# ScalarE's share and order of work in the first row of an attention and mixer kernel, and a float64 conversion by absolute value, limit, shift and sign

## The chip, the cores and the metric

One core of a Trainium2 chip. The metric is the device time of one execution in microseconds (us). The kernel before took 1377.46 us (median of three runs, 1377.15 to 1379.82). "PE" in a profile is TensorE, "PEld" its weight loads, "DVE" VectorE, "ACT" ScalarE, "POOL" GpSimd, "SP" SyncE, which only issues transfers here ("SPq").

## The reference, cut to what matters

```python
# q, k, v: (8, 8, 576, 64) float32; tau = 0.02
scores = np.matmul(q, k.transpose(0, 1, 3, 2)) / 8.0
thresh = np.max(scores, axis=-1, keepdims=True) - tau
scores = np.where(scores >= thresh, scores, -1e9)
attn = softmax(scores)                       # along the last axis
x = (attn @ v) -> (B=8, S=576, H*D=512)      # heads side by side
# mixer; its weights are float64
u = x + (relu(x^T @ w_tok1) @ w_tok2)^T      # 576 -> 256 -> 576
out = u + relu(u @ w_ch1) @ w_ch2            # 512 -> 1536 -> 512
```

The reference's weights are float64, the kernel works in float32. So the kernel also converts each weight itself, from the two 32-bit words of a float64.

## The kernel before

The kernel goes over the attention in iterations `u`, nine to a pair of head pairs, 18 to a batch row. The first row (u = 0 to 17) has nothing else for TensorE to do; later rows fill TensorE's gaps with the mixer of the row before. In iteration `u` it computes scores of `u`, normalizes `u-1` and turns (transposes) unit `u-2`. The first row's turns are made by TensorE, nine blocks of 128x128 in three thirds, into PSUM tiles that share two banks:

```python
def turn(u, third):
    ...
    ps = ps_tr.tile(...)                       # two banks, three thirds
    for c in range(3):
        nc.tensor.transpose(out=ps[:, c, :], in_=e[:, k0 : k0 + P], identity=ident)
    on = nc.scalar.copy if third == 1 and u % 2 else nc.vector.tensor_copy
    on(out=eTs[key][:, 3 * third : 3 * third + 3, ...], in_=ps)
```

Every third iteration of the first row (u = 5, 8, 11, 14, 17) also multiplies three turned units with the values ("iterations with values"; the others I call plain). One iteration in the order of the program, cut:

```python
scores(u)                        # TensorE; then VectorE's maxima, GpSimd's bias
...
    last = values_due(u)         # TensorE, in iterations with values
norm(u - 1)                      # VectorE's reciprocal, GpSimd's scaling
weight_to(2.25 * (u - 1.5))      # conversion steps (first row)
while copies: copies.popleft()() # VectorE copies the values' result to xT
for i in range(3): turn(w, i)    # w = u - 2
...
weigh(u)                         # ScalarE: Prelu with the threshold, Exp
weight_to(2.25 * (u - 1))        # conversion steps
if t in when: load_qk(...)       # issue loads of q and k for later heads
if t == 2: prep(n + 1)           # VectorE transposes q and k (also at t == 7)
```

The conversion is cut into 31 pieces of three steps. A step has work for ScalarE (two steps), VectorE (three), GpSimd (an addition of the two words), and it issues the load of a later piece:

```python
def on_scalar(i, part):   # lo, hi: the two words of each float64
    part 0: lo = int(lo * 2^-29)                  # lower word, rounded
    part 1: h2 = Square(hi as float32)
def on_vector(i, part):
    part 0: bits = (hi << 3) & 0x3FFFFFFF         # tensor_scalar
    part 1: bits = (hi & 0xC0000000) | bits       # two tensors
    part 2: dst  = (h2 >= 2^-30) * dst            # two tensors
def weight(n):            # for each of the next n steps
    if part == 0: on_gpsimd(i - 1); load_piece(i - 1 + NRAW)
    else:         on_scalar(i + 1, part - 1)
    on_vector(i, part)
```

## Time and profile before

| what | before |
|---|---|
| time | 1377.46 us |
| TensorE busy after 200 us | 974 of 980 us |
| TensorE busy in the first 200 us | 157 of 200 us |
| second row starts (scores of u = 18) | 104.20 us |

The slices, the table by stretch and the timelines that the argument starts from are shown in the prediction. The conversion's VectorE work on full pieces (columns: line, engine, operation, tiles, forms, count | busy us, mean ns | idle just before, and what ended most of it):

```profile
L205 DVE SCALAR_TENSOR_TENSOR wc<-scratch,wc 128x512 uint32<-128x512 uint32 x24 | 24.2, 1009 | 0.6
L209 DVE SCALAR_TENSOR_TENSOR wc<-h,wc 128x512 f32<-128x512 f32 x24 | 20.0, 832 | 1.1
L201 DVE TENSOR_SCALAR wc<-scratch 128x512 uint32<-128x512 uint32 x24 | 14.2, 590 | 1.8 <-DMA scratch<-in_moe_w_ch_dram 1.8
```

The means lie far above the medians that the prediction quotes (702, 692 and 412 ns for all 26 full pieces): the same step takes up to 1.7 us when GpSimd works at the same time. Three waits between 14 and 200 us (columns: who, for whom: us in total, times, longest):

```profile
ACT eT L355 <- PE tr L353: 23.2, 7, 6.1
PE tr L353 <- DVE eT L355: 17.7, 8, 3.6
DVE mx L307 <- PE sc L302: 10.5, 10, 2.2
```

The second is TensorE's transposes that wait until VectorE has copied a turn's third out of the bank they need. The first is ScalarE idle before its copies, the third VectorE idle before its maxima.

### The profile page before, as it was taken

What the parts mean: (1) busy time and instruction counts of PE and PEld (TensorE: products, weight loads), DVE (VectorE), ACT (ScalarE), POOL (GpSimd) and SP (SyncE); (2) the same over time, 40 slices, a digit from 0 to 9 for tenths busy, and PEclk for the clock granted to TensorE, in tenths of its full rate; (3) what the DMA queues carried; (4) which work ended last, traced back from release to release, by engine and by line L of the source; (5) the groups of instructions that cost most, each with busy time, mean ns of one, the idle gap of its engine ahead of it and who ended that gap; (6) DMA issues with size and microseconds to landing.
All of it is one profiled execution on the core that took longest, in us unless ns stands there. A gap on an engine that the chain in (4) does not pass through costs nothing.

```text
span 1375.1 us, 17691 instructions
## 1 busy us (share of the span) xinstructions
PE 1322.7 (96%) x6226; PEld 817.9 (59%) x6226; DVE 588.2 (43%) x1017; ACT 581.8 (42%) x1288; POOL 356.0 (26%) x683
## 2 busy tenths in 40 slices
PE   6877799999999999999999999999999999999998
PEld 3444465646565666565665567565656576575675
DVE  6788875445444443434244444434333453201000
ACT  5666654454445444443434444353333444120110
POOL 4555653222222222222122222222121222100000
PEclk9988999999999999999999999999999999999999
DMA  5434655454544354433344435434433442400000
GB/s 121 98 96 125 183 142 124 100 123 98 122 109 114 82 121 94 113 88 95 77 100 94 113 77 123 106 83 98 103 87 75 107 103 63 115 1 16 8 11 21
DMA packets 278871, 128.20 MB, mean 93 GB/s; under 512 B 200896, under 2 KB 271552, under 8 KB 278784
## 3 DMA queue, kind: packets, MB, share of 16 engines
q1 hardware_dynamic: 150176, 111.06, 32.0%
q10 hardware_dynamic: 128608, 16.01, 7.3%
q8 instruction: 50, 0.82, 0.3%
q14 instruction: 37, 0.30, 0.1%
HBM read 43.25 MB, written 9.44 MB: 38 GB/s over the span
## 4 chain that ended last, share of the span: by engine, by line
PE 85%; DVE 7%; DMA 2%; SPq 2%; ACT 1%; issue 1%; POOL 1%; ACTq 0%; DVEq 0%; POOLq 0%
PE c L486 26%; PE c L470 26%; PE sc L302 11%; PE pv L413 9%; PE t L441 5%; PE t L448 3%; PE pv L408 3%; DVE mx L307 2%; SPq L374 2%; PE tx L432 1%; PE c L482 1%; DMA eT<-T 1%; PE tr L353 1%; DVE wc L205 1%; ACT e L317 1%
## 5 line engine op out<-in xcount | busy, mean ns | idle before, releaser
L307 DVE TENSOR_REDUCE mx<-sc 128x1 f32<-128x576 f32 x288 | 204.5, 751 | 487.9 <-PE sc L302 487.5
L470 PE MATMUL c<-xT,wc 128*128 128x256 f32 (+1 forms) x1920 | 399.4, 362 | 2.1 <-DVE xT L452 1.2
L486 PE MATMUL c<-wc,g 128*128 128x512 f32 x864 | 390.5, 597 | 0.0
L470 PEld LDWEIGHTS c<-xT,wc 128*128 128x128 f32 x1920 | 334.5, 191 | 71.5 <-issue 27.6
L308 POOL TENSOR_SCALAR bias<-mx,toff 128x1 f32<-128x1 f32 x288 | 82.8, 288 | 799.3 <-DVE mx L307 742.3
L317 ACT ACTIVATE e<-sc,bias 128x576 f32<-128x576 f32 x288 | 199.6, 739 | 162.0 <-POOL bias L308 161.4
L486 PEld LDWEIGHTS c<-wc,g 128*128 128x128 f32 x864 | 157.8, 190 | 175.7 <-issue 174.0
L471 ACT ACTIVATE g<-c 128x256 f32<-128x256 f32 (+1 forms) x240 | 86.7, 362 | 334.1 <-PE c L470 317.9
L324 ACT ACTIVATE e<-e,ntau 128x576 f32<-128x576 f32 x288 | 220.7, 771 | 0.0
L335 POOL TENSOR_SCALAR e<-e,rr 128x576 f32<-128x576 f32 x288 | 215.6, 761 | 15.8 <-DVE rr L332 4.3
L302 PE MATMUL sc<-kT,qT 64*128 64x288 f32 (+1 forms) x1280 | 196.6, 447 | 11.1 <-DVE kT L284 7.1
L365 DVE STREAM_TRANSPOSE T<-e 128x1152 f32<-128x1152 f32 x126 | 172.1, 1366 | 6.3 <-DMA eT<-T 2.6
L302 PEld LDWEIGHTS sc<-kT,qT 64*128 64x128 f32 (+1 forms) x1280 | 107.4, 184 | 98.3 <-issue 59.1
L413 PE MATMUL pv<-eT,lv 128*64 128x384 f32 (+1 forms) x1024 | 136.8, 409 | 0.0
L413 PEld LDWEIGHTS pv<-eT,lv 128*64 128x64 f32 x1024 | 76.1, 138 | 51.0 <-issue 43.6
L491 DVE COPY o<-c 128x512 f32<-128x512 f32 x36 | 24.9, 692 | 177.5 <-PE c L486 177.5
L418 ACT COPY xT<-pv 128x384 f32<-128x384 f32 (+1 forms) x56 | 21.0, 401 | 157.5 <-PE pv L413 157.5
L448 PE MATMUL t<-w,a 128*128 128x288 f32 x256 | 75.2, 421 | 7.2 <-DVE xT L452 5.3
L441 PE MATMUL t<-x_sb,w 128*128 128x512 f32 x160 | 72.1, 598 | 0.0
L448 PEld LDWEIGHTS t<-w,a 128*128 128x128 f32 x256 | 45.6, 191 | 32.2 <-issue 11.4
L452 DVE TENSOR_TENSOR xT<-xT,t 128x288 f32<-128x288 f32 x64 | 28.2, 446 | 80.5 <-PE t L448 80.0
L324 ACT ACTIVATION_READ_ACCUMULATOR e<-e,ntau 128x1 f32 x288 | 56.5, 196 | 0.0
(44 smaller groups left out, 554.7 us busy)
## 6 DMA issues: line engine op xcount, KB each, us to landing
eT<-T SPq DMA_DIRECT2D x672, 108.0 KB, 2.2
scratch<-in_moe_w_ch_dram SPq DMA_DIRECT2D x24, 512.0 KB, 3.7
lv<-in_v_dram SPq DMA_DIRECT2D x32, 288.0 KB, 3.3
out_dram<-o SPq DMA_DIRECT2D x36, 256.0 KB, 2.2
lk<-in_k_dram ACTq DMA_DIRECT2D x111, 72.0 KB, 2.6
lq<-in_q_dram ACTq DMA_DIRECT2D x106, 72.0 KB, 2.3
lq<-in_q_dram SPq DMA_DIRECT2D x22, 72.0 KB, 3.2
lk<-in_k_dram SPq DMA_DIRECT2D x17, 72.0 KB, 3.3
```

The lines of the kernel that those rows point to most:

```text
L302: nc.tensor.matmul(sc[h][rows, f, 0:HS], lhsT=qT[r, cols], rhs=kT[r, HS * f : HS * f + HS], start=True, stop=True)
L307: nc.vector.tensor_reduce(out=mx[:, c], in_=sc[h][:, :, 0:HS], axis=AX.XY, op=ALU.max)
L317: nc.scalar.activation(out=eh, in_=sc[h][:, :, 0:HS], func=AF.Prelu, bias=bias[:, h : h + 1], scale=SCALE, alpha=STEEP)
L324: nc.scalar.activation(out=eh, in_=eh, func=AF.Exp, bias=ntau, accum_out=rs[:, h : h + 1])
L335: nc.gpsimd.tensor_scalar(out=eh, in0=eh, scalar1=rr[:, h : h + 1], scalar2=1.0, op0=ALU.mult, op1=ALU.mult)
L365: nc.vector.transpose(out=T[:, :, place, :].rearrange("p a (c x) -> p c a x", c=NK), in_=e.rearrange("p (c a x) -> p c a x", c=NK, a=4))
L413: nc.tensor.matmul(to[r], lhsT=lv[:, j, :], rhs=e[j], start=False, stop=(c == NI - 1), skip_group_check=True)
L441: nc.tensor.matmul(ps, lhsT=w1[:, t, P * m : P * m + P], rhs=x_sb[:, t, :], start=(t == 0), stop=(t == NT - 1))
L448: nc.tensor.matmul(ps, lhsT=s["a"][:, m, P * c : P * c + P], rhs=w2[:, m, HS * f : HS * f + HS], start=(m == 0), stop=(m == NTK - 1))
L470: nc.tensor.matmul(ps, lhsT=wc1[:, j, c, :], rhs=uT[:, c, GR * i : GR * i + n], start=(c == 0), stop=(c == NCC - 1))
L471: nc.scalar.activation(out=s["g"][:, j, 0:n], in_=ps, func=AF.Relu)
L486: nc.tensor.matmul(flat, lhsT=s["g"][:, j, P * t : P * t + P], rhs=wc2[:, j, :], start=False, stop=(j == NJ - 1), skip_group_check=True)
```

## The change

Three parts. (a) ScalarE copies the middle third of every turn, not only of odd units. (b) In the first row's iterations with values, more conversion steps and ScalarE's Prelu and Exp stand ahead of the turns in the program, so that these engines work while TensorE multiplies the values. (c) The conversion is done another way: absolute value of the upper word (ScalarE), limit from below and multiply by 2^16, shift by 3, then put the sign in. It has one two-tensor step where it had two. The prediction's (d) is a consequence of (c): VectorE's first step of a piece now needs ScalarE's result.

```diff
@@ on_scalar
-                nc.scalar.activation(out=h2, in_=hi.bitcast(F32), func=AF.Square)
+                nc.scalar.activation(out=h2, in_=hi.bitcast(F32), func=AF.Abs)
@@ on_vector
             if part == 0:
+                nc.vector.tensor_scalar(out=h2, in0=h2, scalar1=2.0**-15, scalar2=2.0**16, op0=ALU.max, op1=ALU.mult)
+            elif part == 1:
                 nc.vector.tensor_scalar(
-                    out=bits, in0=hi, scalar1=3, scalar2=0x3FFFFFFF, op0=ALU.logical_shift_left, op1=ALU.bitwise_and
+                    out=bits, in0=h2.bitcast(U32), scalar1=3, scalar2=0, op0=ALU.logical_shift_left, op1=ALU.bitwise_or
                 )
-            elif part == 1:
-                nc.vector.scalar_tensor_tensor(
-                    out=bits, in0=hi, scalar=0xC0000000, in1=bits, op0=ALU.bitwise_and, op1=ALU.bitwise_or
-                )
             else:
-                nc.vector.scalar_tensor_tensor(out=dst, in0=h2, scalar=2.0**-30, in1=dst, op0=ALU.is_ge, op1=ALU.mult)
+                nc.vector.scalar_tensor_tensor(
+                    out=bits, in0=hi, scalar=0x80000000, in1=bits, op0=ALU.bitwise_and, op1=ALU.bitwise_or
+                )
@@ turn
-        on = nc.scalar.copy if third == 1 and u % 2 else nc.vector.tensor_copy
+        on = nc.scalar.copy if third == 1 else nc.vector.tensor_copy
@@ main loop
+        visit = False
         if due and not in_blocks(due[0][1]):
+            visit = due[0][0] <= u
             last = values_due(u)
...
-            weight_to(2.25 * (u - 1.5))
+            weight_to(2.25 * (u - (1 if visit else 1.5)))
+            if visit and on:
+                weigh(u)
...
-        if on:
+        if on and (b_now or not visit):
             weigh(u)
```

## The prediction

> **What bounds the kernel now.** I read the page's slices first, to see where TensorE is not full; then a table by stretch; then TensorE's timeline and waits inside the stretch that is not full; then VectorE's and ScalarE's timelines of single iterations.
>
> ```profile
> PE   6877799999999999999999999999999999999998
> DVE  6788875445444443434244444434333453201000
> PEclk9988999999999999999999999999999999999999
> ```
>
> Each digit is a slice of 34.4 us. TensorE is at 9 from the sixth slice on, and VectorE is high only before that. The same by stretch (columns: window, then busy us of PE, PEld, DVE, ACT, POOL, then PE clock, DMA share, GB/s):
>
> ```profile
> 0.00:104.00 104.00, 78.73 (x444) 47.77 (x444) 77.20 (x165) 64.75 (x135) 55.00 (x101) 0.92 0.46 104
> 104.00:125.00 21.00, 14.95 (x65) 8.32 (x63) 18.62 (x33) 15.46 (x31) 11.82 (x15) 0.67 0.58 147
> 125.00:200.00 75.00, 63.39 (x310) 40.82 (x307) 65.45 (x97) 46.82 (x97) 45.92 (x52) 0.98 0.58 154
> 200.00:1180.00 980.00, 974.35 (x4662) 597.23 (x4661) 416.05 (x708) 432.54 (x969) 243.26 (x518) 1.00 0.44 100
> ```
>
> After 200 us TensorE is busy 974 of 980 us: VectorE or ScalarE time saved there is worth nothing. All the change can win lies in the first 200 us, where TensorE idles 43 us (25.3 + 6.1 + 11.6) and runs below full clock. That caps the gain: 2% of 1377.5 is 27.5 us, nearly two thirds of all that idle time. The first row (18 iterations, turned on TensorE) ends at about 120 us; the weights' conversion ends at 200.
>
> What TensorE waits for in the first row (start, length, engine, what, idle before and what ended it), here seven last transposes of a turn:
>
> ```profile
> 29.60 0.55 PE L353 MATMUL tr<-ident,e 128*128 128x128 f32 x3 [2.31 <-DVE eT L355]
> 42.12 0.55 PE L353 MATMUL tr<-ident,e 128*128 128x128 f32 x3 [1.32 <-DVE eT L355]
> ...
> 55.13 0.55 PE L353 MATMUL tr<-ident,e 128*128 128x128 f32 x3 [0.57 <-ACT eT L355]
> 60.87 0.55 PE L353 MATMUL tr<-ident,e 128*128 128x128 f32 x3 [3.03 <-DVE eT L355]
> 74.25 0.55 PE L353 MATMUL tr<-ident,e 128*128 128x128 f32 x3 [2.18 <-DVE eT L355]
> ...
> 90.45 0.55 PE L353 MATMUL tr<-ident,e 128*128 128x128 f32 x3 [0.57 <-ACT eT L355]
> 95.96 0.90 PE L353 MATMUL tr<-ident,e 128*128 128x128 f32 x3 [2.53 <-DVE eT L355]
> ```
>
> The turns' PSUM has two banks and a turn has three thirds, so the last third waits for an earlier copy. Where ScalarE copies the middle third (odd units), the wait is 0.57 us and it is ScalarE's copy that ends it: the last third takes the middle one's bank. Where VectorE makes all three (even units), the wait is 1.3 to 3.0 us, because VectorE gets to its first copy only after two maxima, the sum's reciprocal and a conversion step. Seven plain even iterations wait 0.44 + 2.31 + 1.32 + 3.03 + 2.18 + 2.53 + 2.33 = 14.1 us.
>
> The iterations with values are different: there VectorE and ScalarE wait for TensorE, and do what could have been done meanwhile afterwards. The end of the last one:
>
> ```profile
> 103.90 0.48 ACT L355 COPY eT<-tr 128x384 f32<-128x384 f32 x1 [5.83 <-PE tr L353]
> 104.28 1.38 ACT L317 ACTIVATE e<-sc,bias 128x576 f32<-128x576 f32 x2
> 104.78 0.68 DVE L205 SCALAR_TENSOR_TENSOR wc<-scratch,wc 128x512 uint32<-128x512 uint32 x1
> 105.57 0.69 DVE L209 SCALAR_TENSOR_TENSOR wc<-h,wc 128x512 f32<-128x512 f32 x1
> 106.18 1.42 DVE L307 TENSOR_REDUCE mx<-sc 128x1 f32<-128x576 f32 x2
> ```
>
> ScalarE idles 5.8 us before its copy with its two Prelu behind it, though their bias was ready; VectorE puts two steps between its last copy and the next maxima, which are on the loop.
>
> **What the Trainium skill says.** "VectorE: DVE Perf Modes", section "The perf-mode tier table": fp32 `tensor_scalar` from SBUF to SBUF reaches two results a cycle, two-tensor work one. The trace agrees, on bit operations too: a 128x512 TENSOR_SCALAR has a median of 412 ns, SCALAR_TENSOR_TENSOR 702 and 692.
>
> "SBUF — State Buffer", section "Who interferes with whom": VectorE and GpSimd share a port pair, held for a whole instruction, wanted by two-input operations and by the two-port mode. The trace fits: the same three steps take up to 1516, 1676 and 1600 ns beside GpSimd's work. So the cheaper step does not escape the lock.
>
> "ScalarE: Activation LUTs", section "Table sets": abs is filler in every set, so no table load. Square takes 661 ns (median); the page has one rate for all functions, so I expect the same for the absolute value.
>
> "TensorE: Matmul & The Clock Gate", section "What's actually happening": idling lowers the clock, activity releases it. The trace shows 0.67 to 0.92 where TensorE idles and 1.00 after. Less idling may thus also shorten the matmuls; I count little for it, since when it switches cannot be read from here.
>
> **The change part by part.**
>
> (a) ScalarE copies the middle third in every turn: nine copies of 0.55 us leave VectorE (nominally 5 us), nine of 0.48 us go to ScalarE. The larger effect is the bank: the last third then follows ScalarE's early copy as in odd units. The seven waits would shrink to 0.57 each: 14.1 - 4.0 = 10.1 us of TensorE idle removed. But the loop then runs at VectorE's pace. Per even iteration VectorE loses the middle copy (about 0.5) and the gap before the last copy (0.17 to 0.53), plus what it waits for scores that now come earlier (0 to 0.6): about 1.0 us each, 7 us in all. I take 7, not 10.
>
> (b) Work ahead of the turns, in five iterations with values. In the one shown the next maxima can start when their first scores are there, about 105.3 instead of 106.18: 0.9. After the first one I read 0.8 in the same way; the one at 61 has one step of 0.42 less: 0.4; the one at 79 has a step of 0.68 behind a middle copy of 0.5, but the scores come at 88.5 against maxima at 89.17: 0.65; the one at 46 about 0.5. Sum 3.3. ScalarE's earlier Prelu frees the score banks sooner; the scores right after odd such iterations take 2.05 to 2.11 us, where others at full clock take 1.25. This overlaps with the same loop, so it adds perhaps 0.3: 3.6.
>
> (c) Conversion: Square becomes Abs (no cost), a bit TENSOR_SCALAR becomes one with max and multiply (0.41 for 0.41), one SCALAR_TENSOR_TENSOR of 0.69 becomes a TENSOR_SCALAR of 0.41, the other stays. So 0.28 us for each of 26 full pieces and about 0.15 for the five small ones: 8 us of VectorE time. In the first row the shortened step is on the loop in about five plain iterations: 5 x 0.28 = 1.4, of which I keep 1. In the second row (18 pieces, 5 us) half falls into the lock behind GpSimd's addition: 1.
>
> (d) What it adds: VectorE's first step now needs ScalarE's Abs, where it needed only the load. In the first row Abs mostly comes a call earlier: no wait that I can find. From the second row on Abs and the first step are in the same call, and ScalarE then often stands behind a Relu that waits for TensorE. At 148.70 the step would wait for an Abs that ends at about 149.1, and an addition that TensorE waits 2.19 us for stands behind it: 0.3 to 0.4 lost. Two or three of these: -1.
>
> Sum: 7 + 3.6 + 1 + 1 - 1 = 11.6 us. 1377.5 - 11.6 = 1366, -0.8%.
>
> **The rivals.**
>
> R1, VectorE's throughput takes the place of the wait. It is already busy 77 of the first 104 us and 84 of the next 96. If the even iterations merely trade the wait at the last third for a wait at the next scores or maxima, (a) is worth its nine copies at most where VectorE has no slack, some 3 us, and the whole about 6: 1371. For it: VectorE often runs without a gap from the last copy to the next maxima. Against it: the removed copy and the removed gap both lie in that very run.
>
> R2, the new dependency costs more than it gives: VectorE is in order, so a late Abs also delays maxima, copies and the additions that TensorE waits for. With 1 us lost in each of the nine second-row iterations that convert, the gain falls to about 4: 1373. For it: ScalarE waits 13.6 us there for weight loads, and VectorE did not wait for most of those. Against: the delayed step often would have stood in the lock anyway (the one after it takes 1.66 us where GpSimd's addition runs), so a delay there is partly free.
>
> R3, the clock joins in: with shorter gaps the first row stays at full clock. An iteration with values that ran at 0.78 took 7.9 us, the one at 1.00 took 6.6, with much the same work. Four of them a us faster, plus (a) at its full 10: 1358.
>
> R4, nothing: gains end in the wait for weight loads before 200 us, as these are issued behind VectorE's transposes' 16 DMAs on one queue. Against it: those loads move forward with the steps that issue them. 1376.
>
> **Range and chances.** R1 and R2 pull to 1371-1373, R3 to 1358. I take 1366, with 1358 to 1374 for eight in ten. Faster by over 2% would need 1350 or less, so two thirds of the idle time in 200 us: 0.03. Slower by over 2% would need 27 us of new waits in a stretch where each is bounded by a few: 0.005. The rest, 0.965, is within 2%.
>
> **What would show it.** (a) is right if no last third of a plain even turn waits over 1 us for VectorE's copy, and the wait of transposes for VectorE's copies (17.7 us on TensorE) falls below 8. (b) is right if ScalarE's 23.2 us of waiting before its copies goes to where its Prelu are already done, and the maxima follow the last copy with no step between them. (c) is right if the two TENSOR_SCALAR have a median near 0.41 us and the full conversion's VectorE time falls by about 8 us. (d) is right if VectorE waits for Abs under 4 us in all. After 200 us (less the gain) nothing may differ. The prediction is wrong if the first iteration of the second row starts less than 6 or more than 15 us earlier than before (104.2 us), or if what is won there is lost again before TensorE is full.

## The result, and the profile after

The changed kernel takes 1372.28 us (median of six runs, 1370.45 to 1375.01); the kernel before took 1379.57 in the same rounds (six runs, 1377.15 to 1383.88). The ratio is 0.9946, 95% interval 0.9924 to 0.9967: within 2%. The ratios here are worked out from the runs of the same rounds. They are not quite the ratios of the medians or of the plain means (for no_a below, the plain means give 0.9969). At -0.54% the gain is 7.4 us of the 11.6 predicted. The time lies inside the range, 6 us above its middle.

The trace taken with that result is of the slowest of its six runs, and in it the first scores start at 8.88 us against 7.06 before, because a first load landed late. A second set of runs (whole_again, below) gave a trace that starts at 7.06 us like the one of before. I use that second trace: span 1366.8 us against 1375.1. It is of the fastest of its six runs (1368.63 us), and the trace of before is of a run (1376.94 us) as fast as that kernel's fastest, so both show a somewhat better case than the medians do. Its slices of 34.2 us:

```profile
PE   6877899999999999999999999999999999999998
DVE  5878764445453543434334354434333443201000
PEclk9999999999999999999999999999999999999999
```

TensorE's fifth slice is at 8 where it was at 7, and the clock no longer falls to 8. By stretch, in the prediction's windows and columns:

```profile
0.00:104.00 104.00, 76.99 (x463) 48.44 (x463) 78.28 (x169) 75.19 (x157) 58.78 (x105) 0.98 0.48 111
104.00:125.00 21.00, 15.36 (x72) 8.69 (x72) 17.86 (x29) 13.37 (x27) 13.00 (x15) 0.84 0.56 158
125.00:200.00 75.00, 63.82 (x303) 40.11 (x302) 56.92 (x96) 45.87 (x97) 40.29 (x53) 1.00 0.59 155
200.00:1180.00 980.00, 974.22 (x4688) 597.31 (x4687) 413.26 (x700) 429.00 (x963) 240.40 (x512) 1.00 0.43 99
```

After 200 us nothing differs: TensorE is busy 974.22 us where it was 974.35. In the first 104 us TensorE does more work (463 instructions in the trace where there were 444) in less busy time, because its clock is 0.98 where it was 0.92, and ScalarE is busy 75.2 us where it was 64.8. The second row starts 6.07 us earlier (in the first trace, of the slowest run, at 103.68 us and so only 0.52 us earlier):

```profile
98.13 2.07 PE L303 MATMUL sc<-kT,qT 64*128 64x288 f32 x8
```

The last thirds of the plain even turns, which waited 0.4 to 3.0 us for VectorE, now wait for ScalarE's copy: 0.57 us in four of the seven, 0.82 to 1.37 us in three, 5.8 us in all for 14.1 before (shown are iterations 4, 6, 10, 12 and 16; line numbers are one higher than before):

```profile
27.86 0.55 PE L354 MATMUL tr<-ident,e 128*128 128x128 f32 x3 [0.82 <-ACT eT L356]
38.62 0.55 PE L354 MATMUL tr<-ident,e 128*128 128x128 f32 x3 [0.57 <-ACT eT L356]
...
56.94 0.55 PE L354 MATMUL tr<-ident,e 128*128 128x128 f32 x3 [1.37 <-ACT eT L356]
66.81 0.55 PE L354 MATMUL tr<-ident,e 128*128 128x128 f32 x3 [0.57 <-ACT eT L356]
...
87.80 0.55 PE L354 MATMUL tr<-ident,e 128*128 128x128 f32 x3 [1.33 <-ACT eT L356]
```

The waits between 14 and 200 us, those that answer to the three of before and the new one for the absolute value:

```profile
DVE mx L308 <- PE sc L303: 16.5, 10, 4.4
...
ACT eT L356 <- PE tr L354: 13.0, 10, 2.8
...
PE tr L354 <- ACT eT L356: 10.2, 12, 1.4
...
DVE h L202 <- ACT h L194: 8.6, 4, 4.0
...
PE tr L354 <- DVE eT L356: 5.0, 1, 5.0
```

TensorE's wait for VectorE's copies fell from 17.7 us to 5.0 (and that one is in the second row), while its wait for ScalarE's copies grew from 3.1 to 10.2. VectorE's wait for scores grew from 10.5 us to 16.5, but most of that in the second row: up to 125 us it grew from 5.5 to 7.4. And the conversion's VectorE work:

```profile
L208 DVE SCALAR_TENSOR_TENSOR wc<-scratch,wc 128x512 uint32<-128x512 uint32 x24 | 19.8, 824 | 0.4
L204 DVE TENSOR_SCALAR wc<-h 128x512 uint32<-128x512 uint32 x24 | 17.1, 713 | 0.7
L202 DVE TENSOR_SCALAR h<-h 128x512 f32<-128x512 f32 x26 | 15.8, 609 | 8.6 <-ACT h L194 8.6
```

All the conversion's steps together took VectorE 70.7 us between 14 and 200 us before, and 63.2 now. ScalarE's step costs the same (median 671 ns for Abs, 662 for Square), and both traces have one table load, as the prediction expected.

The length of iterations, from one scores' start to the next (iteration 2 from the second half of its scores), summed by kind:

| iterations | before | after | |
|---|---|---|---|
| plain, even (2, 4, 6, 10, 12, 16) and 18 | 37.80 us | 28.48 us | -9.3 |
| plain, odd (3, 7, 9, 13, 15) and 19 | 27.53 us | 27.79 us | +0.3 |
| with values (5, 8, 11, 14, 17) | 38.23 us | 40.38 us | +2.2 |

So the even iterations gave more than the 7 us I had put on part (a), and the iterations with values, on which part (b) works, became longer; iteration 17 alone, with 2.5 us, makes more than all of that. But single traces of this kernel differ by some 3 us in this stretch (first loads land between 7.06 and 8.9 us, clocks differ), so which part does what has to come from times.

### The profile page after: what moved, and what is told of

Same layout as the page of the kernel before. It is cut to its first block, busy times and chain, and to the rows that moved or that the text cites. A ratio compares the mean times of both kernels' runs of the same rounds, so it can differ in the third digit from the quotient of the medians. Undisturbed runs are those within 1.5% of the kernel's fastest.

```text
span 1373.2 us, 17692 instructions
## 1 busy us (share of the span) xinstructions
PE 1320.2 (96%) x6226; PEld 817.9 (60%) x6226; DVE 575.9 (42%) x1008; ACT 586.0 (43%) x1297; POOL 354.6 (26%) x683
## 4 chain that ended last, share of the span: by engine, by line
PE 86%; DVE 5%; DMA 3%; SPq 2%; ACT 1%; issue 1%; POOL 1%; ACTq 0%; DVEq 0%; POOLq 0%
PE c L471 26%; PE c L487 26%; PE sc L303 11%; PE pv L414 9%; PE t L442 5%; PE t L449 3%; PE pv L409 3%; DVE mx L308 2%; SPq L375 2%; PE tx L433 1%; PE c L483 1%; DMA eT<-T 1%; PE tr L354 1%; DMA lk<-in_k_dram 1%; DVE wc L208 1%
## 5 line engine op out<-in xcount | busy, mean ns | idle before, releaser
L303 PE MATMUL sc<-kT,qT 64*128 64x288 f32 (+1 forms) x1280 | 193.2, 441 | 12.5 <-DVE kT L285 8.9
```

The source lines that it names most:

```text
L303: nc.tensor.matmul(sc[h][rows, f, 0:HS], lhsT=qT[r, cols], rhs=kT[r, HS * f : HS * f + HS], start=True, stop=True)
```

## The experiments

Twelve kernels ran, each in six runs (a_last_third in five), in three sets of rounds, each set on one chip. All gave correct results.

| kernel | parts | median us | before, same rounds | ratio | 95% interval |
|---|---|---|---|---|---|
| whole_again | a b c | 1371.64 | 1379.44 | 0.9937 | 0.9914 to 0.9960 |
| a_only | a | 1374.64 | 1379.44 | 0.9960 | 0.9936 to 0.9984 |
| b_only | b | 1382.52 | 1379.44 | 1.0010 | 0.9984 to 1.0036 |
| c_only | c | 1377.06 | 1379.44 | 0.9978 | 0.9956 to 1.0001 |
| no_a | b c | 1374.35 | 1378.76 | 0.9976 | 0.9958 to 0.9993 |
| no_b | a c | 1371.03 | 1378.76 | 0.9942 | 0.9930 to 0.9954 |
| no_c | a b | 1375.05 | 1378.76 | 0.9974 | 0.9959 to 0.9988 |
| abs_early | a b c, ScalarE's steps earlier | 1374.63 | 1378.76 | 0.9969 | 0.9956 to 0.9981 |
| a_last_third | a on another third | 1394.34 | 1381.68 | 1.0098 | 1.0080 to 1.0115 |
| load_first | a b c, one load earlier | 1370.76 | 1381.68 | 0.9920 | 0.9898 to 0.9941 |
| both_early | a b c, load and copies earlier | 1370.48 | 1381.68 | 0.9918 | 0.9902 to 0.9934 |
| ac_both_early | a c, load and copies earlier | 1370.87 | 1381.68 | 0.9925 | 0.9908 to 0.9942 |

### Each part alone

The theory was my own sum (a 7, b 3.6, c and d 1 together); the rivals were that VectorE's pace takes (a) away, that (b) does nothing, and that the new dependency costs more. The whole, unchanged:

> The change once more, to have it in the same rounds as its parts, and a second trace, as the first one was taken of the slowest of its runs (its first scores came 1.8 us late, on a load). Expected: -7 us against the kernel before (ratio 0.995). If the trace starts as early as that of before, the first scores of the second row should come 3 to 6 us earlier than 104.2.

Measured: 0.9937, beside 0.9946 in the first rounds; so the whole gains 0.54 to 0.63%, 7.4 to 8.7 us.

Part (a) alone is the kernel before with one line changed:

```diff
-        on = nc.scalar.copy if third == 1 and u % 2 else nc.vector.tensor_copy
+        on = nc.scalar.copy if third == 1 else nc.vector.tensor_copy
```

> Only ScalarE's copy of the middle third in every turn. Theory BANK (a as predicted): the seven last thirds of even plain turns stop waiting for VectorE; -4 to -7 us. Rival PACE (VectorE's rate takes the wait's place): -1 to -3 us. A cost of its own: in iterations with values ScalarE's Prelu now stands behind the copy in all five, not in three, so the gain may be lower than with the reordering.

Measured: 0.9960, so -0.40%, 5.5 us. Less than 7 and more than the 3 of the rival. In its trace the even iterations take 33.0 us for 37.8 before, and the odd ones 22.4 for 19.0 (3, 7, 9, 13 and 15). So part of what the removed waits gave came back, but not as the rival had it: 3.2 of these 3.4 us are in iterations 9 and 15, which follow the two even iterations with values (8 and 14). It is the cost that was expected besides: ScalarE now waits there for the middle third, and its Prelu stand behind that copy. Iteration 8 in a_only:

```profile
52.74 0.48 ACT L355 COPY eT<-tr 128x384 f32<-128x384 f32 x1 [3.55 <-PE tr L353]
53.03 2.11 PE L302 MATMUL sc<-kT,qT 64*128 64x288 f32 x8
53.11 1.38 ACT L317 ACTIVATE e<-sc,bias 128x576 f32<-128x576 f32 x2
```

Before, the Prelu of iteration 8 started at 50.09 us, ahead of the turn, and the next scores took 1.25 us for these 2.11. In the changed kernel, where (b) puts the Prelu ahead of the turns, both iterations are back at 3.1 us (4.2 and 5.2 in a_only).

Part (b) alone is the kernel before with the four edits of the main loop in the diff above (`visit`, `weight_to`, and `weigh(u)` twice):

> Only the reordering in the five iterations with values. As predicted: -3.6 us. If the middle copy on ScalarE is what makes it pay, or if the steps moved ahead fall into GpSimd's lock before the copies, it is 0 to -2.

Measured: 1.0010, with 1.000 well inside its interval. The 3.6 us of the prediction (0.9974) lie outside it. How this came is read below.

Part (c) alone is the kernel before with the edits of `on_scalar` and `on_vector`:

> Only the conversion by absolute value. As predicted (c and d): -1 us. If the wait for Abs costs more (8.8 us of VectorE's time in the changed kernel's trace after 104 us), +1 to +3 us; if that wait only stands in the place of others, -2 to -3.

Measured: 0.9978, so -0.22%, 3 us, with 1.000 just inside its interval.

### All parts but one

To see whether parts overlap or help each other, the change with one part undone. The diffs are those above, backwards.

> The change without ScalarE's copy in even turns. If the parts simply add up (alone they gave -0.4%, +0.1% and -0.2%), this gives -0.1%, -1.5 us. If a is needed for b to pay (even turns then hold VectorE's loop), no less; if b is worth something only beside a, about -3 us would speak for it being c alone.

> The change without the reordering. Adding up: -0.6% (-8.5 us), as much as the whole or a little more; then b was worth nothing at all. If b serves a (as ScalarE's copy now stands before Prelu in every iteration with values), less: -5 us.

> The change with the old conversion. Adding up: -0.3% (-4 us). If c is needed, as three steps in one call take 0.28 us less each in iterations with values, -3; if b pays beside a, -6.

Measured: 0.9976, 0.9942 and 0.9974. With these, each part has four pairs of kernels that differ in it alone (for the whole I take the mean of its two measurements, 0.99415; some pairs compare ratios from different sets of rounds, and so from different chips):

| part | on nothing | on one other | on one other | on both others | mean |
|---|---|---|---|---|---|
| a | -0.40 | -0.36 (on b) | -0.36 (on c) | -0.35 | -0.37% |
| b | +0.10 | +0.14 (on a) | -0.02 (on c) | -0.01 | +0.05% |
| c | -0.22 | -0.18 (on a) | -0.34 (on b) | -0.33 | -0.27% |

In us of 1379.6: (a) -5.1, (b) +0.7, (c) with its dependency (d) -3.7; the sum is -8.1, and the whole measured -7.4 to -8.7. Each mean is good to about 0.15% or 2 us (an estimate: the intervals' half widths are 0.12 to 0.26%, and a mean is made of eight such ratios). So, as far as these intervals tell, the parts add up, each is worth the same whatever stands beside it, and (b) is worth nothing: the change without (b) is as fast as the whole. That the times add up does not mean that the traces do; see the end of the next section.

### Why part (b) gives nothing

Two things are in the trace of b_only. First, what the shorter path from the last copy to the next maxima is worth. In the iteration after the first one with values the kernel before has (scores, and VectorE's maxima of them, after two conversion steps):

```profile
37.96 2.05 PE L302 MATMUL sc<-kT,qT 64*128 64x288 f32 x8
...
39.70 1.42 DVE L307 TENSOR_REDUCE mx<-sc 128x1 f32<-128x576 f32 x2 [0.22 <-issue]
```

and with (b), where the two steps are done earlier:

```profile
37.98 1.25 PE L302 MATMUL sc<-kT,qT 64*128 64x288 f32 x8
38.08 0.56 DVE L355 COPY eT<-tr 128x384 f32<-128x384 f32 x1 [0.64 <-PE tr L353]
39.73 1.42 DVE L307 TENSOR_REDUCE mx<-sc 128x1 f32<-128x576 f32 x2 [1.08 <-PE tr L353]
```

The maxima start at 39.73 us, after a wait of 1.08 us, where they started at 39.70 without it. The steps stood in time that VectorE had to wait anyway. (The profile puts this wait down to a transpose behind the scores; why the maxima do not start at 39.3 is not clear.) From the scores' start to the maxima's the five iterations that follow one with values took 1.74, 1.34, 2.26, 1.34 and 1.98 us before, and 1.75, 1.34, 1.93, 1.34 and 1.34 with (b). At full clock 1.34 us is what eight score matmuls take before the maxima can start, and two iterations were already there. What is won is 0.33 + 0.64 = 1.0 us, where the prediction had 3.3.

Second, what it costs. A step moved ahead of the turns also stands ahead of VectorE's copy of the values' result, which TensorE waits for. Iteration 8 before:

```profile
50.90 0.61 DVE L420 COPY xT<-pv 128x192 f32<-128x192 f32 x2
...
51.66 0.92 PE L353 MATMUL tr<-ident,e 128*128 128x128 f32 x6 [0.47 <-DVE xT L420]
```

and in b_only:

```profile
51.05 0.47 DVE L209 SCALAR_TENSOR_TENSOR w<-h,w 128x288 f32<-128x288 f32 x1
51.44 0.61 DVE L420 COPY xT<-pv 128x192 f32<-128x192 f32 x2
...
52.20 0.92 PE L353 MATMUL tr<-ident,e 128*128 128x128 f32 x6 [1.10 <-DVE xT L420]
```

The copy starts 0.54 us later (0.72 counted from the iteration's start) and TensorE waits 1.10 us where it waited 0.47. In that trace the five iterations with values take 40.2 us for 38.2 before, but 1.4 of these 2.0 us are in iteration 17, where TensorE waits 0.34 us for the copy as before and one group of its matmuls takes 2.59 us for 1.47 at a lower clock (0.50 and 0.66 where it was 0.85 and 1.00). So alone (b) wins about 1 us behind these iterations, and what it surely loses in them is less than 1.

Beside (a), and so in the changed kernel, both sides are larger. Iterations 6, 9, 12 and 15, which follow one with values, take 17.9 us in no_b and 12.4 in whole_again; the five with values take 36.1 and 40.4. With the two mends described further below it is the same (17.9 and 12.4, 33.2 and 38.3 us in ac_both_early and both_early). From the scores' start to the maxima's hardly anything changes there: 6.29 and 5.95 us for the four in no_b and whole_again. So the gain is not the steps that the prediction counted. The trace of a_only above suggests ScalarE's earlier Prelu, which the prediction put at 0.3 us; no run separates them. About as much is lost again in the iterations with values, into which the work was moved.

### Is it the bank, or VectorE's relief?

My step for (a) rested on the bank: the last third takes the middle third's bank. A rival says that only VectorE's nine copies matter. To tell them apart I let ScalarE copy the last third in even turns instead, which relieves VectorE as much and leaves the bank with VectorE's first copy:

```diff
-        on = nc.scalar.copy if third == 1 and u % 2 else nc.vector.tensor_copy
+        on = nc.scalar.copy if third == (1 if u % 2 else 2) else nc.vector.tensor_copy
```

> The kernel before, but in even turns ScalarE copies the last third in place of none: VectorE gets the same relief as by a alone (nine copies of 0.55 us), and the last third's bank still comes from VectorE's first copy. Theory BANK: the waits of 1.3 to 3 us in even turns stay, and the gain is a third of that of a alone or less (0 to -2 us). Rival PACE (the relief is what counts): as a alone, -4 to -6.

Measured: 1.0098, slower by 13 us. TensorE's transposes still waited 14.5 us (8 times) for VectorE's copies, so that wait does hang on whose copy frees the bank. But the slowdown has another cause, which makes it no clean test of the pace:

```profile
32.00 0.55 PE L353 MATMUL tr<-ident,e 128*128 128x128 f32 x3 [1.46 <-DVE eT L355]
...
32.47 3.56 PE L302 MATMUL sc<-kT,qT 64*128 64x288 f32 x8
...
32.58 0.48 ACT L355 COPY eT<-tr 128x384 f32<-128x384 f32 x1 [3.42 <-PE tr L353]
...
32.95 1.38 ACT L317 ACTIVATE e<-sc,bias 128x576 f32<-128x576 f32 x2
```

ScalarE, which works in order, idles 3.42 us until the late last third is there, its Prelu stand behind that copy, and the scores, whose banks the Prelu free, take 3.56 us. What relief of VectorE is worth with the bank left alone stays open; a kernel in which ScalarE copies the middle third and VectorE does as much other work would show it.

### Is the wait for the absolute value what costs?

In the changed kernel VectorE waits 8.6 us (four times) for ScalarE's Abs; I had predicted under 4. If this costs, doing ScalarE's two steps one step earlier should win:

```diff
-            else:
-                on_scalar(i + 1, part - 1)
+            elif part == 1:
+                on_scalar(i + 1, 1)
+                on_scalar(i + 1, 0)
```

> The change with ScalarE's two conversion steps issued together one step earlier, so that VectorE's first step does not follow Abs in the same call. It tests d. VectorE waited 8.8 us for Abs in the changed kernel's trace. If that wait cost what was predicted (1 us) or was free because GpSimd's lock stood behind it, 0 to -1 us against the change; if it cost most of itself, -4 to -6 us against the change, -12 against before.

Measured: 0.9969, against 0.9937 and 0.9946 for the change: not faster, rather 0.3% slower, though in other rounds. Its waits between 14 and 200 us:

```profile
ACT h L194 <- DMA scratch<-in_moe_w_ch_dram: 17.0, 6, 6.7
...
DVE h L202 <- ACT h L194: 3.4, 1, 3.4
...
ACT h L194 <- DMA lq<-in_q_dram: 3.3, 1, 3.3
```

VectorE's wait fell from 8.6 us to 3.4 as intended, and the time did not follow. ScalarE waits 17.0 us at this step for the weights' load; in the change it waited 18.0 us for it at its other step, which came first there. So taking most of the wait away won nothing. That the wait was free is likely but not shown, as the edit also moved ScalarE's steps and may have added a cost of its own.

### A load that stands behind a waiting load

Iteration 17 is the one that lost most: 7.41 us before, 9.86 in the second trace of the change. There (GpSimd's addition, SyncE's issues, VectorE, TensorE):

```profile
85.95 1.46 POOL L216 TENSOR_TENSOR wc<-wc,scratch 128x512 int32<-128x512 int32 x1
...
87.43 0.39 SPq L177 DMA_DIRECT2D scratch<-in_moe_w_ch_dram  x1
...
87.87 0.49 SPq L105 DMA_DIRECT2D lq<-in_q_dram  x1
...
91.66 0.78 DVE L285 STREAM_TRANSPOSE qT<-lq 128x576 f32<-128x576 f32 x1 [1.58 <-issue]
...
96.52 0.61 DVE L421 COPY xT<-pv 128x192 f32<-128x192 f32 x2
...
97.28 0.92 PE L354 MATMUL tr<-ident,e 128*128 128x128 f32 x6 [3.69 <-DVE xT L421]
```

SyncE issues the weights' load at 87.43, when GpSimd's addition (done at 87.41) frees its buffer. The last loads of q and k stand behind it in SyncE's program and go out at 87.87 and 88.41, and VectorE's transpose of q waits 1.58 us before it starts (0.40 before the change; the profile names nothing that ended this wait, hence "issue", so the load is a theory here); maxima, conversion steps, the values' copy and TensorE follow behind. If that is the cause, issuing the q and k load ahead of the weights' load takes it away:

```diff
+            if t == 6:
+                load_qk(n + 2, (nc.sync, nc.sync), range(6, 8))   # then weight_to(2.25 * (u - 1))
...
-            if t in when:
+            if t in when and (b_now or t != 6):
```

> The whole change, with the last q and k load of the first row issued ahead of the weight load that waits for GpSimd. Theory LOAD (the last iteration with values is 2.5 us longer than before, as its transposes of q and k wait for a load that stands behind a weight load): -2 us against the change, -9 to -10 against before. If the scores or the value copies set that iteration anyway: as the change, -7 to -8.

Measured: 0.9920. In its trace VectorE's transpose follows the step before it without a wait:

```profile
90.05 0.77 DVE L285 STREAM_TRANSPOSE qT<-lq 128x576 f32<-128x576 f32 x1
...
93.89 1.03 DVE L208 SCALAR_TENSOR_TENSOR wc<-scratch,wc 128x512 uint32<-128x512 uint32 x1
94.84 0.61 DVE L421 COPY xT<-pv 128x192 f32<-128x192 f32 x2
```

Iteration 17 takes 8.12 us for 9.86. The order of issue was the cause of that wait. TensorE's wait for the values' copy shrinks from 3.69 to 1.97 us but not to before's 0.34: three conversion steps still stand ahead of the copy, the last of them 1.03 us beside GpSimd. That is part (b) once more.

A second such place is iteration 14, where TensorE waits for GpSimd's copies of the values' middle columns, which stand behind its addition:

```profile
73.38 1.45 POOL L216 TENSOR_TENSOR wc<-wc,scratch 128x512 int32<-128x512 int32 x1
...
74.78 0.99 POOL L382 COPY vl<-lv 64x64 f32<-64x64 f32 x2
...
75.53 1.15 PE L409 MATMUL pv<-eT,vl 128*64 128x384 f32 x4 [2.26 <-POOL vl L382]
```

The kernel both_early is load_first with these copies two iterations earlier (their condition on the turned unit is `wt % GU == 0` where it was `wt % GU == GU - 1`):

> As load_first, and GpSimd's copies of the values' middle columns two iterations earlier, so that they do not stand behind its norm and addition when TensorE wants the values (waits of 2.3 and 0.5 us in the changed kernel). If they set that iteration: -2 us against load_first. If VectorE's maxima set it: no difference.

Measured: 0.9918, beside 0.9920 for load_first on the same chip. The wait is gone and iteration 14 takes 7.95 us for load_first's 9.12, and yet the time does not move. A gain of 1.2 us is less than these intervals can tell (half widths of 0.16 and 0.22%, 2 to 3 us), so whether this wait was on the path stays open. Last, both mends without part (b), since (b) is where these waits grew:

> Parts a and c without the reordering b, with both of these mends: the version meant to beat both kernels. Without b the change gave -0.58% as with it. The load did not stop VectorE there, GpSimd's copies cost TensorE 2.7 us: -0.7 to -0.8% (-10 us). If b is worth something once the load is out of its way, both_early is the better of the two by 1 to 3 us.

Measured: 0.9925, the same as with (b) within the intervals. The three mended kernels gain 0.75 to 0.82% on the kernel before, the change 0.54 to 0.63% in other rounds, and the intervals overlap. So they beat the kernel before; that they beat the change is likely from the mended wait but not shown.

## Why the prediction was right or wrong

The time was right (1372.28 in 1358 to 1374), and so was the class. By its own steps:

- **What bounds, and the cap.** Right: all that differs lies in the first 200 us.
- **(a), 7 us.** The mechanism is right: the last thirds wait for ScalarE's early copy, only one wait for VectorE's copy is left (5.0 us, under the 8 set), and no last third of a plain even turn waits for VectorE. The size is 5.1 us with an uncertainty of 2, so 7 is at its edge. Two things took from it: waits for ScalarE's copy of 1.3 to 1.4 us, where the copy stands behind Exp and a conversion step in ScalarE's order, and, without (b), iterations 9 and 15, as ScalarE's Prelu came late. The prediction's own doubt, VectorE's pace, is not what the trace of a_only shows.
- **(b), 3.6 us: the step that failed.** The prediction says that in the iteration shown "the next maxima can start when their first scores are there, about 105.3 instead of 106.18", and reads the four others the same way. It took VectorE's conversion steps to be all that held the maxima. They need the scores, 1.34 us after these start at the earliest, and in three of five iterations the steps filled just that time: 1.0 us was to be had, not 3.3. It put ScalarE's earlier Prelu at 0.3 us, when beside (a) the iterations behind those with values shrink by some 5.5. And it counted the moved work as leaving the path, when it moved ahead of the values' copy, which is on the path as well: there 4 to 5 us are lost again. Measured +0.7, with an uncertainty of 2. The check I had written ("the maxima follow the last copy with no step between them") holds and proves nothing: a wait took the step's place.
- **(c), 2 us, and (d), -1.** The count was right: VectorE's conversion time fell by 7.5 us where 8 was said, and the two TENSOR_SCALAR have medians of 0.43 and 0.44 us, near the 0.41 predicted. The terms of the sum were mis-sized: together 3.7 us, not 1. For (d), the wait is longer than predicted (8.6 us, not under 4), but taking most of it away won nothing. Where (c) wins cannot be read from single traces: by the starts of iterations 2 and 18, the first row is 1.9 us longer with it and 4.4, 3.5 and 2.8 us shorter in the four pairs of kernels, 2.2 shorter on average, where I had 1 (for the whole I take the mean of its two traces). The clocks of these traces differ too: between 14 and 104 us it is 0.88 in no_c and 0.98 in whole_again. Which waits (c) shortens stays open.
- **The rivals.** R1 (VectorE's pace) came nearest in time, 1371, but not for its reason: what came back from (a) in the trace of a_only is ScalarE's lateness, as read above. Its 3 us for (a) are at the lower edge of 5.1 with an uncertainty of 2. R2 (dependency) falls with (c)'s gain, which includes (d). R4 falls: the gain reaches the end.
- **R3, the clock, is not settled.** Its 1358 was not reached, but a part of the gain may have come this way. The mean granted clock of the runs is 0.9885 in the kernel before and 0.9917 in whole_again, of the same rounds. Over 1375 us that is 4.3 us at full clock of the 8.7 gained (an estimate, and rather an upper one, as TensorE is not busy all the time). Split by parts as the times were, it is 3.3 us for (a), 0.0 for (b) and 2.6 for (c), of 5.1, -0.7 and 3.7. The prediction counted little for the clock. No run here holds it fixed, so how much of (a) and (c) is a removed wait and how much a clock that fell less often stays open.

By the prediction's own sign of being wrong, a second row that starts less than 6 us earlier, it just passes in the second trace (6.07 us) and fails in the first (0.52 us, or 2.3 if the late first scores are taken off). In all, 11.6 was 7 + 3.6 + 1; it should have been 5.1 - 0.7 + 3.7. So that the time fell into the range is partly luck: the range held any gain from 3.5 to 19.5 us, and what (b) did not give, (c) made good in part.

## What to carry to other kernels

To remove work between a result and its consumer helps only as far as the consumer's other input is ready: find out when that comes, before you count the time as won. Work moved forward in an in-order engine's program lands ahead of something else, so look for what it now delays, a copy that another engine waits for or a load behind a load. And run each part of a change alone and left out: here a part with no value travelled unnoticed with two that had some. Last, compare the granted clocks of the two kernels before you put a gain down to a removed wait alone.

## What the Trainium skill lacked or had wrong

- "DMA: Bandwidth & Descriptors", section "Issuing engines are not separate DMA queues", says that spreading issues over engines only saves the issue's own time, usually small. The section does not go on to say that an issue which waits for its buffer holds up the later issues of the same engine: here 1.58 us of VectorE's wait, gone when the two loads changed places.
- "SBUF — State Buffer", section "Who interferes with whom", tells who takes the lock but gives no size for short steps. Here the single-input steps with medians of 0.43 and 0.44 us have means of 0.61 and 0.69 us over the 26 full pieces (most of them overlap GpSimd's work) and take up to 1.5 us; even so the cheaper steps kept 7.5 of the 8 us that their undisturbed durations promise.
- No page that I looked up speaks of three PSUM tiles in two banks, where the engine that makes an early copy decides how long a late tile waits: TensorE's waits for VectorE's copies were 17.7 us with one choice and 5.0 us with the other.
